# Casting loads in natural order, split first loads and a refitted schedule in a block-sparse attention kernel with a squared-ReLU MLP

## The chip, the cores and the metric

The kernel runs on one core of a Trainium2 chip. The metric is the device time of one launch in microseconds, lower is better; it is the median of three runs. The engines are TensorE (PE; its weight loads are listed as PEld), VectorE (DVE), ScalarE (ACT), GpSimd (POOL) and SyncE (SP), which here only issues DMAs. TensorE writes to PSUM, and DVE and ACT evacuate it from there.

## The reference

Two parts follow each other. The first is block-sparse attention over 4 batches x 8 heads, 768 tokens and head size 64; a query block of 32 tokens sees its neighbours, the first and the last block, three sampled blocks, and the first and last query block see everything. The second takes the 3072 x 512 result through two matrices with a squared ReLU between.

```python
scores = scale * np.matmul(q, k.transpose(0, 1, 3, 2))        # 4 x 8 x 768 x 768
...                                                            # mask from blocks of 32
scores = np.where(mask, scores, -1000000000.0)
attn = np.exp(scores - max)                                    # cut: the row maximum
attn = attn / (np.sum(attn, axis=-1, keepdims=True) + 1e-09)
x = np.matmul(attn, v)        # then heads side by side: 3072 x 512
...
h = x @ w_in                  # 3072 x 2048
r = np.maximum(h, 0.0)
out = (r * r) @ w_out         # 3072 x 512
```

## The kernel before

Heads are worked on in pairs: 16 pairs (u), four to a batch. A pair's q, k and v come as float32 of 384 KB each. For the first four pairs (batch 0) q and k are cast to bf16 by an engine (tile `qc`, with the two heads of a chunk of 128 tokens side by side), transposed on TensorE (tile `pt`) and evacuated to `QK`. For later pairs a DMA transposes them.

```python
    N_WARM = 12
    NRAW, NPB, QC_BUFS, XQ_BUFS = 4, 6, 5, 4
...
    sy.dma_start(out=sb_i, in_=sampled_blocks.bitcast(I32))
    load(0, (sy, sc_, sy))        # queues of q, k, v
    load(1, (sc_, sy, sc_))
    load(2, (sy, sc_, sy))
    load(3, (sc_, sy, sy))
...
    for _ in range(N_WARM):
        nc.tensor.matmul(junk, warm[:, 0:P], warm, start=True, stop=True)
...                               # POOL: iotas, one-hot rows oh, identity; DVE: mask bm
    def cast_qk(u, w, ns, e):
        c = work.tile([P, NCH, 2, D], BF, name="qc", tag="qc", bufs=QC_BUFS)[:, ns]
        copy(e, c, raw[u][w].rearrange("p t n d -> p n t d")[:, ns])

    def transp(u, w, ns, e):
        src = cast.pop((u, w, ns.start))
        pt = ps_h.tile([P, NCH, P], BF, name="pt", tag="h")
        for i, n in enumerate(range(ns.start, ns.stop)):
            nc.tensor.transpose(pt[:, n], src[:, i].rearrange("p t d -> p (t d)"), identb)

    def evac(u, w, ns, e):
        copy(e, QK[u % NPB][:, w]..., ttile.pop((u, w, ns.start))[:, ns])     # cut
```

A unit of attention is a slot: a pair, 256 queries and 256 keys. TensorE makes the scores (`ps`), two heads at once in two halves of the array's rows. ACT takes the exponential into `pT`. DVE multiplies by the 0/1 mask `MK`, and TensorE multiplies by v (`po`). The first twelve slots do without `MK`: TensorE adds mask rows (`R2`, evacuated from `pb`) to their scores. `MK` is made on TensorE (`pk`) in tiles of 512 and 256 columns.

```python
    def exps(a, e):
        A.activation(out=pT, in_=stile.pop(a), func=AF.Exp, scale=scale)
    def masks(a, e):
        V.tensor_tensor(out=pT, in0=pT, in1=m[:, None].broadcast_to([P, 2, 2, QW]), op=AOP.mult)
```

The result of a slot row is normalized on DVE (`rs`, `xq`), transposed to `xT`, and goes through the second part: `ph` (hidden), relu to `r` on DVE or ACT, square to `g` on GpSimd or ACT, `py` (output), copy to `ys`, store.

```python
    def hidden(T, f, half, e):                                   # ph: 4 matmuls of 256 or 384 columns
            nc.tensor.matmul(ph, w_in_sb[:, kc, f * P:(f + 1) * P], xT[b][:, kc, c0:c0 + w], ...)
    def output(T, ts, part, e):                                  # py: 16 matmuls of 512 columns
            nc.tensor.matmul(py, gtile[T, f][:, ts * P:(ts + 1) * P], w_out_sb[:, f, :], ...)
    def out_copy(T, ts, e):
        ys = work.tile([P, d_model], F32, name="ys", tag="ys", bufs=3)
        copy(e, ys, ytile.pop((T, ts)))
    def store(T, ts, e):
        sy.dma_start(out=ov[T[0], :, T[1] // P + ts, :], in_=ystile.pop((T, ts)))
```

No order of instructions is written by hand. While the program is built, `run_schedule` takes tasks with assumed durations, arrivals of loads and hand-over times, picks for each step the task that can start first, chooses its engine where more than one is allowed, and so fixes the order on every engine.

```python
    LAT = {"PE": 0.23, "DVE": 0.06, "ACT": 0.06, "POOL": 0.08, "SP": 2.0}
    SWITCH = 0.1
    AHEAD = {"PE": 0.05, "DVE": 0.2, "ACT": 0.25, "POOL": 0.0, "SP": 0.0}
    LEAD = 12.0
    PACE0, PACE, SINGLE, MASK_AT = 40.0, 1.6, 1, 12.0
...
    arrive = [(6.2, 6.2, 8.4), (8.4, 10.5, 10.5), (12.5, 12.5, 13.6), (13.6, 15.2, 16.3)]   # q, k, v of pairs 0 to 3
```

Of the kernel before, what the change touches and what calls it, by code (L numbers as in the profile page):

```python
# [19 lines left out]
P = 128  # L20
# [5 lines left out]
def kernel(  # L26
# [31 lines left out]
    N_WARM = 12  # L58
    NRAW, NPB, QC_BUFS, XQ_BUFS = 4, 6, 5, 4
# [19 lines left out]
    SWITCH = 0.1  # L79
    AHEAD = {"PE": 0.05, "DVE": 0.2, "ACT": 0.25, "POOL": 0.0, "SP": 0.0}  # L80
    LEAD = 12.0
    PACE0, PACE, SINGLE, MASK_AT = 40.0, 1.6, 1, 12.0
# [18 lines left out]
    def run_schedule(free, bufs, dma_free, mode=128):  # L101
        taken = {name: [] for name in bufs}
        port = {"DVE": (0.0, 0.0), "POOL": (0.0, 0.0)}
        waiting = list(tasks)
        ready = []

        def seen(d, eng):
            late = d.late if d.late is not None else (0.0 if d.eng == eng else LAT[d.eng])
            return d.end + late

        while waiting or ready:
# [6 lines left out]
            for t in ready:  # L118
# [15 lines left out]
                for e, us in t.engs.items():  # L134
                    r = max([r0, free[e]] + [seen(d, e) for d in t.deps])
                    sw = SWITCH if e == "PE" and t.mode and t.mode != mode else 0.0
                    if e == "POOL" or (e == "DVE" and t.port):
                        p0, p1 = port["DVE" if e == "POOL" else "POOL"]
                        us += 0.7 * max(0.0, min(r + us, p1) - max(r, p0))
# [12 lines left out]
            if e == "POOL" or (e == "DVE" and t.port):  # L152
                port[e] = (at, end)
            if e == "PE" and t.mode:
                mode = t.mode
# [34 lines left out]
    sy, sc_ = nc.sync, nc.scalar  # L190
    sb_i = consts.tile([nb, n_rand * 2], I32, name="sb_i")
    sy.dma_start(out=sb_i, in_=sampled_blocks.bitcast(I32))
    load(0, (sy, sc_, sy))
    load(1, (sc_, sy, sc_))
    load(2, (sy, sc_, sy))
    load(3, (sc_, sy, sy))
# [24 lines left out]
    G.iota(row, pattern=[[0, 1]], base=0, channel_multiplier=1, **small)  # L221
    o3 = oh.rearrange("a (n p) -> a n p", p=P)
# [12 lines left out]

    edge = consts.tile([nb, 2], F32, name="edge")
# [11 lines left out]
    A.copy(out=oh[D:P, :], in_=oh[0:D, :])  # L248
# [13 lines left out]
    def mask_rows(e):  # L262
        mtile["R"] = ps_s.tile([P, 1024], F32, name="pb", tag="ps")
        for c0 in (0, 512):
            w = min(512, S - c0)
            nc.tensor.matmul(mtile["R"][:, c0:c0 + w], bm, oh[0:nb, c0:c0 + w], start=True, stop=True)

    def mask_rows_evac(c0, c1, e):
        copy(e, R2[:, c0:c1], mtile["R"][:, c0:c1])
# [27 lines left out]
    def transp(u, w, ns, e):  # L297
        src = cast.pop((u, w, ns.start))
        pt = ps_h.tile([P, NCH, P], BF, name="pt", tag="h")
        for i, n in enumerate(range(ns.start, ns.stop)):  # L300
            nc.tensor.transpose(pt[:, n], src[:, i].rearrange("p t d -> p (t d)"), identb)  # L301
# [9 lines left out]
    held = consts.tile([1, 2], F32, name="held")  # L311
# [6 lines left out]
    def w_load(i, e):  # L318
        if i == 0:
            G.tensor_copy(out=held, in_=raw[2][1][0:1, 0, 0, 0:2])  # L320
# [127 lines left out]
    def y_pool(T, ts):  # L448
        return "h" if T == TILES[-1] and ts % 2 else "y"

    def output(T, ts, part, e):
        if part == 0:
            pool, tag = (ps_h, "h") if y_pool(T, ts) == "h" else (ps_y, "y")
            ytile[T, ts] = pool.tile([P, d_model], F32, name="py", tag=tag)
        py = ytile[T, ts]
        for f in range(part * NF // NY, (part + 1) * NF // NY):
            nc.tensor.matmul(py, gtile[T, f][:, ts * P:(ts + 1) * P], w_out_sb[:, f, :],  # L457
                             start=(f == 0), stop=(f == NF - 1))

    def out_copy(T, ts, e):  # L460
        ys = work.tile([P, d_model], F32, name="ys", tag="ys", bufs=3)
        copy(e, ys, ytile.pop((T, ts)))
        ystile[T, ts] = ys

    def store(T, ts, e):
        sy.dma_start(out=ov[T[0], :, T[1] // P + ts, :], in_=ystile.pop((T, ts)))
# [6 lines left out]
    arrive = [(6.2, 6.2, 8.4), (8.4, 10.5, 10.5), (12.5, 12.5, 13.6), (13.6, 15.2, 16.3)]  # L473
# [9 lines left out]
    def prepare(u):  # L483
# [5 lines left out]
        if u >= HP:  # L489
            g = gate[2] if u == HP else gate[5] if u == HP + 1 else gate[7]  # L490
            ld_t = T_(("SP", 1.3), s0 - 30, load, u, (sy, sy, sy),
                      deps=cv[u - NRAW] + tr[u - NRAW] + [g], dma=4.0)
# [7 lines left out]
        else:  # L500
            at = dict(after=arrive[u][2])
            for ns in (slice(0, 2), slice(2, NCH)) if u == 0 else (slice(0, NCH),):
                n = ns.stop - ns.start
                for w in (0, 1):
                    qc, hb = Buf("qc"), Buf("h")
                    opts = {"ACT": 0.23 + 0.1 * n} if u == 0 and w else {"DVE": 0.07 + 0.08 * n}
                    if u:
                        opts["POOL"] = 1.2
                    c = T_(opts, s0 - 6 + ns.start, cast_qk, u, w, ns, after=arrive[u][w], get=[qc], port=True)
                    tr[u].append(c)  # L510
                    t = T_(("PE", 0.06 * n), s0 - 5 + ns.start, transp, u, w, ns, deps=[c], get=[hb], put=[qc], mode=128)
                    opts = {"DVE": 0.14 + 0.07 * n}
                    if u == 0:
                        opts["ACT"] = 0.23 + 0.1 * n
                    x = T_(opts, s0 - 4 + ns.start, evac, u, w, ns, deps=[t], put=[hb])
                    for j in range(ns.start, ns.stop, 2):
                        ev[u][w, j] = x
            for w in (0, 1):
                ev[u].setdefault((w, 2), ev[u][w, 0])
        cv[u] = [T_({"POOL": 0.83, "DVE": 0.55}, s0 - 2 if u < HP else 101, cast_v, u, bias={"DVE": 0.6},  # L520
                    deps=at.get("deps", []) + old_v, after=at.get("after", 0.0), port=True)]
        if u == HP - 1:
            for i in range(2 * NWP):
                wl[i] = T_(("POOL", 0.85), -50 + i, w_load, i, after=12.6, late=2.2, dma=2.65)
# [3 lines left out]
    def attend(group, add):  # L528
# [4 lines left out]
                + (mr[:1 + (group[0][1] > 0)] if add else []) + sc_all[-1:], get=[bufs[a] for a in group], mode=64,  # L533
                after=PACE0 + PACE * (s - HP * NQ * CP) if s >= HP * NQ * CP else 0.0)
        sc_all.append(sc)
        for a in group:
# [9 lines left out]
            va = T_(("PE", 0.245), s + 2.2, values, a, deps=[ex] + cv[u] + va_all[-1:],  # L546
# [124 lines left out]
```

The softmax here doesn't subtract the row's maximum and nothing guards it: scores larger than these inputs give would overflow.

## Time and profile before

| | before |
|---|---|
| time, median of 3 | 281.56 us (281.35 to 282.2) |
| span of the profiled run | 279.6 us |
| exponential on ACT, 128x1024 | 144 x 1021 ns = 139.2 us busy |
| mask multiply on DVE, 128x1024 | 132 x 815 ns = 105.1 us busy |
| square on GpSimd | 107 x 889 ns = 94.5 us busy |
| first exponential starts | 8.92 us |
| first hidden matmul starts | 30.17 us |
| last matmul ends | 276.04 us |
| TensorE clock granted | full in every slice |

Matmuls are pipelined, so the busy time of TensorE counts overlapping work and a share of 96% doesn't mean that no time is lost; the distance between starts says more. The chain of waits follows the end of the program back from what released each step. An engine named in it is one that the next step had to wait for, or that had itself been busy until then. Idle time of an engine that nobody waits for costs nothing.

### The profile page before, as it was taken

Reading aid. Unit: us, or ns where it says so; the run is one execution under the profiler, and the core shown is the slowest. Engines: PE = TensorE matmul, PEld = TensorE weight load, DVE = VectorE, ACT = ScalarE, POOL = GpSimd, SP = SyncE. Lnnn points to the kernel's source line nnn. Section 1 sums busy time; section 2 is a strip of 40 time slices with the busy share of each in tenths; the row PEclk is TensorE's granted clock in tenths of the full one; section 3 lists DMA queues with packets and bytes.
Section 4 is the critical chain, followed back from the end, with each engine's and each line's share of the span. In section 5 each row is a group of like instructions: output and inputs, shape, how many; then the busy total and the mean of one; then the engine's idle time right before and its main releaser. Section 6 shows DMA issues by size and latency. Waiting matters only on the chain.

```text
span 279.6 us, 7039 instructions
## 1 busy us (share of the span) xinstructions
PE 267.9 (96%) x2834; PEld 155.6 (56%) x2834; DVE 200.4 (72%) x379; ACT 196.5 (70%) x281; POOL 122.1 (44%) x151
## 2 busy tenths in 40 slices
PE   7888899999999998999999999999999999999994
PEld 2565566566666554555555555555556555555541
DVE  6776889898988779986877888877868744344400
ACT  4689889899899799798988889889789501001011
POOL 4570358576434359752114443211120366666610
PEclk9999999999999999999999999999999999999999
DMA  7999997999933784794106314321011010111112
GB/s 249 378 228 207 269 277 239 195 285 258 357 65 83 237 193 120 213 191 106 56 12 115 81 45 111 70 59 49 19 51 56 12 47 38 40 39 38 40 74 76
DMA packets 50379, 36.89 MB, mean 132 GB/s; under 512 B 30891, under 2 KB 47275, under 8 KB 50347
## 3 DMA queue, kind: packets, MB, share of 16 engines
q1 hardware_dynamic: 44762, 30.29, 40.7%
q0 software_dynamic: 4224, 4.19, 9.0%
q10 hardware_dynamic: 1360, 1.97, 2.1%
q8 instruction: 22, 0.36, 0.6%
q14 instruction: 11, 0.08, 0.1%
HBM read 27.26 MB, written 6.29 MB: 120 GB/s over the span
## 4 chain that ended last, share of the span: by engine, by line
PE 78%; DVE 15%; ACT 4%; issue 2%; ACTq 0%; DVEq 0%
PE py L457 27%; PE ph L427 25%; PE po L382 12%; PE ps L349 11%; DVE pT L366 8%; DVE qc L172 3%; ACT pT L359 2%; DVE xq L391 2%; PE junk L213 2%; DVE rs L389 1%; DVE QK L172 1%; PE pt L301 1%; PE ps L353 0%; DVE r L436 0%; DVE xT L172 0%
## 5 line engine op out<-in xcount | busy, mean ns | idle before, releaser
L445 POOL TENSOR_TENSOR g<-r 128x384 bf16<-128x384 f32 (+1 forms) x107 | 94.5, 889 | 128.8 <-DVE r L436 93.0
L359 ACT ACTIVATE pT<-ps 128x1024 bf16<-128x1024 f32 x144 | 139.2, 1021 | 10.8 <-PE ps L349 7.6
L366 DVE TENSOR_TENSOR pT<-pT,MK 128x1024 bf16<-128x1024 bf16 x132 | 105.1, 815 | 9.0 <-ACT pT L359 8.7
L427 PE MATMUL ph<-xT,w_in_sb 128*128 128x384 bf16 (+1 forms) x576 | 107.8, 308 | 0.0
L457 PE MATMUL py<-w_out_sb,g 128*128 128x512 bf16 x384 | 103.5, 379 | 0.0
L427 PEld LDWEIGHTS <-w_in_sb 128*128 128x128 bf16 x576 | 51.1, 97 | 33.3 <-issue 3.4
L436 DVE TENSOR_SCALAR r<-ph 128x384 f32<-128x384 f32 (+1 forms) x80 | 41.9, 525 | 32.9 <-PE ph L427 22.2
L382 PEld LDWEIGHTS <-pT 128*128 128x128 bf16 x1152 | 45.8, 98 | 28.9 <-DVE pT L366 10.9
L382 PE MATMUL po<-VT,pT 128*128 128x65 bf16 x1152 | 56.5, 194 | 3.2 <-DVE pT L366 1.2
L457 PEld LDWEIGHTS <-g 128*128 128x128 bf16 x384 | 34.4, 98 | 25.7 <-issue 1.5
L170 ACT COPY ys<-py 128x512 f32<-128x512 f32 x21 | 12.3, 586 | 50.2 <-PE py L457 50.0
L349 PE MATMUL ps<-QK 64*128 64x256 bf16 x576 | 46.5, 272 | 1.0 <-ACT pT L359 0.8
L349 PEld LDWEIGHTS <-QK 64*128 64x128 bf16 x576 | 22.9, 94 | 21.2 <-issue 17.0
L434 ACT ACTIVATE r<-ph 128x384 f32<-128x384 f32 (+1 forms) x64 | 27.3, 451 | 6.7 <-PE ph L427 6.2
L443 ACT ACTIVATE g<-r 128x384 bf16<-128x384 f32 (+1 forms) x37 | 18.1, 489 | 6.4 <-DVE r L436 5.8
L391 DVE TENSOR_TENSOR xq<-po,rs 128x256 bf16<-128x256 f32 x48 | 20.4, 424 | 1.7
L172 POOL CAST VT<-vs 128x768 bf16<-128x768 f32 x15 | 14.8, 986 | 12.7 <-PE po L382 7.9
L389 DVE RECIPROCAL rs<-po 128x4 f32<-128x4 f32 x48 | 8.6, 179 | 14.9 <-PE po L382 14.7
L172 DVE CAST qc<-qs 128x768 bf16<-128x768 f32 (+2 forms) x15 | 10.2, 683 | 0.7 <-DMA qs<-in_q_dram 0.7
L172 DVE CAST qc<-ks 128x768 bf16<-128x768 f32 x14 | 10.5, 747 | 0.0
L353 PE MATMUL ps<-R,oh 64*128 64x256 bf16 x48 | 5.9, 269 | 0.0
L213 PE MATMUL junk<-warm 128*128 128x512 bf16 x12 | 4.4, 542 | 1.5 <-DVE warm L205 1.5
(52 smaller groups left out, 60.2 us busy)
## 6 DMA issues: line engine op xcount, KB each, us to landing
out_dram<-ys SPq DMA_DIRECT2D x24, 256.0 KB, 2.0
vs<-in_v_dram SPq DMA_DIRECT2D x15, 384.0 KB, 6.6
qs<-in_q_dram SPq DMA_DIRECT2D x14, 384.0 KB, 4.3
ks<-in_k_dram SPq DMA_DIRECT2D x14, 384.0 KB, 6.2
w_in_sb<-in_moe_w_in_dram POOLq DMA_DIRECT2D x4, 512.0 KB, 9.6
w_out_sb<-in_moe_w_out_dram POOLq DMA_DIRECT2D x4, 512.0 KB, 20.1
ks<-in_k_dram ACTq DMA_DIRECT2D x2, 384.0 KB, 6.2
qs<-in_q_dram ACTq DMA_DIRECT2D x2, 384.0 KB, 4.8
```

The source lines that it names most:

```text
L172: (V if e == "DVE" else G).tensor_copy(out=out, in_=in_)
L349: nc.tensor.matmul(ps[:, h, c, :], QK[i][hs, 1, ksl], QK[i][hs, 0, qsl], start=c == 0, stop=not add, skip_group_check=True)
L359: A.activation(out=pT, in_=stile.pop(a), func=AF.Exp, scale=scale)
L366: V.tensor_tensor(out=pT, in0=pT, in1=m[:, None].broadcast_to([P, 2, 2, QW]), op=AOP.mult)
L382: nc.tensor.matmul(po[:, qc, h, :], pT[:, h, c, qc * P:(qc + 1) * P], VT[i][:, h, n, 0:VW], start=(n == 0 and qc == 0 and h == 0), stop=n ...
L391: V.tensor_tensor(out=xq, in0=po[:, :, :, 0:D], in1=rs.broadcast_to([P, 2, 2, D]), op=AOP.mult)
L427: nc.tensor.matmul(ph, w_in_sb[:, kc, f * P:(f + 1) * P], xT[b][:, kc, c0:c0 + w], start=(kc == 0), stop=(kc == KM - 1))
L434: A.activation(out=r, in_=src, func=AF.Relu)
L436: V.tensor_scalar(out=r, in0=src, scalar1=0.0, scalar2=None, op0=AOP.max)
L443: A.activation(out=g, in_=r, func=AF.Square)
L445: (G if e == "POOL" else V).tensor_mul(out=g, in0=r, in1=r)
L457: nc.tensor.matmul(py, gtile[T, f][:, ts * P:(ts + 1) * P], w_out_sb[:, f, :], start=(f == 0), stop=(f == NF - 1))
```

## The change

- Pairs 1 to 3: q and k are no longer cast by engines. DMAs issued by GpSimd cast while they load, into six tiles `nat` that keep the order of memory (head, chunk, 64 values). So the two heads of a chunk don't lie side by side, and TensorE transposes each head's 64 columns by itself, into the upper or lower half of `pt`: twice as many transposes, half as wide. Their v follows on the SP queue, each after a tiny DMA that waits until the pair's q has landed. `qs`, `ks` and `vs` need one buffer less.
- First pair: q and k are loaded in two parts, the first two chunks and then the other four, so that the first scores need a third of the bytes.
- The weights' first load no longer waits for a load of pair 2.
- Last tokens: the output of the last 128 tokens is made in two halves of 256 columns, so that the first half is copied and stored while the second is made.
- Scheduler: nine warm-up matmuls instead of twelve; new arrivals, hand-over times and pace; contention of DVE and GpSimd now lengthens the earlier task too; a slack of 0.1 us where TensorE waits for another engine; squares are kept off ACT more strongly; the evacuation of the later mask rows and the mask tiles of 256 columns move later.

```diff
-    N_WARM = 12
-    NRAW, NPB, QC_BUFS, XQ_BUFS = 4, 6, 5, 4
+    N_WARM = 9
+    NRAW, NPB, QC_BUFS, XQ_BUFS, YS_BUFS = 3, 6, 5, 4, 3
@@ scheduler
-    SWITCH = 0.1
-    AHEAD = {"PE": 0.05, "DVE": 0.2, "ACT": 0.25, "POOL": 0.0, "SP": 0.0}
-    LEAD = 12.0
-    PACE0, PACE, SINGLE, MASK_AT = 40.0, 1.6, 1, 12.0
+    SWITCH, SHARE, SLACK = 0.096, 0.6, 0.1
+    AHEAD = {"PE": 0.03, "DVE": 0, "ACT": 0.1, "POOL": 0.0, "SP": 0.0}
+    LEAD = 8
+    PACE0, PACE, SINGLE, MASK_AT, ADDED = 36, 1.589, 1, 15.0, 0
...
-            return d.end + late
+            return d.end + late + (SLACK if eng == "PE" and d.eng != "PE" else 0.0)
@@ loads
+    def load_first():
...
+        for ns in SPLIT:                  # chunks 0 to 1, then 2 to 5
+            cs = slice(ns.start * D, ns.stop * D)
+            for eng, t, view in ((sy, qs, qv), (sc_, ks, kv)):
+                eng.dma_start(out=t[:, :, ns].rearrange("p t n d -> p t (n d)"), in_=view[0, 0][:, :, cs])
+        sy.dma_start(out=vs.rearrange("p t n d -> p t (n d)"), in_=vv[0, 0])
+
+    def load_cast(u, w):
+        t = consts.tile([P, 2, NCH, D], BF, name=f"nat{u}{w}")
+        G.dma_start(out=t.rearrange("p t n d -> p t (n d)"), in_=(qv, kv)[w][0, u])
+
+    def load_v(u, e):
+        sy.dma_start(out=scratch[0:1, u:u + 1], in_=nat[u, 0][0:1, 0, 0, 0:1])
+        t = ld.tile([P, 2, NCH, D], F32, name="vs", tag="vs")
+        sy.dma_start(out=t.rearrange("p t n d -> p t (n d)"), in_=vv[0, u])
...
-    load(0, (sy, sc_, sy))
-    load(1, (sc_, sy, sc_))
-    load(2, (sy, sc_, sy))
-    load(3, (sc_, sy, sy))
+    load_first()
...                                        # POOL: after the iotas
+    load_cast(1, 0)
+    load_cast(1, 1)
...                                        # POOL: after one-hot rows, identity, ones of VT
+    for u in range(2, HP):
+        for w in range(2):
+            load_cast(u, w)
@@ transposes
-            nc.tensor.transpose(pt[:, n], src[:, i].rearrange("p t d -> p (t d)"), identb)
+            if u == 0:
+                nc.tensor.transpose(pt[:, n], src[:, i].rearrange("p t d -> p (t d)"), identb)
+            for t in range(2) if u else ():
+                nc.tensor.transpose(pt[t * D:(t + 1) * D, n], src[:, t, n], identb)
@@ weights
-        if i == 0:
-            G.tensor_copy(out=held, in_=raw[2][1][0:1, 0, 0, 0:2])
@@ last tokens
+    HALVES = ((0, d_model // 2), (d_model // 2, d_model))
...
+        return ys[:-1] + [(n - 1, cs) for cs in HALVES] if T == TILES[-1] else ys
@@ tasks
-    arrive = [(6.2, 6.2, 8.4), (8.4, 10.5, 10.5), (12.5, 12.5, 13.6), (13.6, 15.2, 16.3)]
+    arrive = [(4.6, 4.6, 8.2), (7.6, 9.1, 12.3), (10.4, 12.1, 15.0), (13.5, 14.8, 17.0)]
...
-                wl[i] = T_(("POOL", 0.85), -50 + i, w_load, i, after=12.6, late=2.2, dma=2.65)
+                wl[i] = T_(("POOL", 0.85), -50 + i, w_load, i, after=9.5 + 1.5 * i, late=2.2, dma=2.65)
...
-            va = T_(("PE", 0.245), s + 2.2, values, a, deps=[ex] + cv[u] + va_all[-1:],
+            va = T_(("PE", 0.245), s + 3.2, values, a, deps=[ex] + cv[u] + va_all[-1:],
...
-            for c0, c1, at in ((QW, S, MASK_AT), (0, QW, 26.0)):
+            for c0, c1, at in ((QW, S, MASK_AT), (0, QW, 38.0)):
...
-                rr = T_(RELU[w], 200, relu, t, f, deps=[h1], get=[rb], put=[hb], bias={"ACT": 0.4})
-                sq_of[x] = T_(SQ[w], n_key, square, t, f, deps=[rr], get=[gb], put=[rb], bias={"ACT": 0.5})
+                rr = T_(RELU[w], 200, relu, t, f, deps=[h1], get=[rb], put=[hb], bias={"ACT": 0.3})
+                sq_of[x] = T_(SQ[w], n_key, square, t, f, deps=[rr], get=[gb], put=[rb], bias={"ACT": 0.9})
```

## The prediction

> **What bounds the kernel now.** I read the share of busy time first, then busy time in stretches, then the chain of waits for the first 31 us, then the order of time around the start and the end. The page's first part and the stretches:
>
> ```profile
> PE 267.9 (96%) x2834; PEld 155.6 (56%) x2834; DVE 200.4 (72%) x379; ACT 196.5 (70%) x281; POOL 122.1 (44%) x151
> ```
>
> ```profile
> 20.00:25.00 5.00, 4.60 (x75) 2.78 (x74) 2.88 (x6) 4.87 (x7) 0.00 (x0) 1.00 1.25 209
> 25.00:30.00 5.00, 3.71 (x65) 2.26 (x61) 4.24 (x10) 3.92 (x7) 0.00 (x0) 1.00 1.20 229
> ...
> 80.00:100.00 20.00, 20.00 (x250) 12.76 (x250) 15.82 (x34) 17.30 (x23) 7.17 (x9) 1.00 0.50 134
> ...
> 200.00:250.00 50.00, 50.00 (x405) 27.67 (x404) 29.52 (x56) 21.41 (x31) 22.27 (x26) 1.00 0.13 41
> ```
>
> The columns of a stretch are its length, then PE, PE weight load, DVE, ACT and GpSimd with their counts, the clock, the DMA share and GB/s. From about 80 us on TensorE is full. What the kernel can gain without removing matmuls lies in the first 30 us, in some holes between 30 and 125 us, and after the last matmul. Two chains of waits and one piece of the timeline show the sizes (start, length, what):
>
> ```profile
> 1.53 4.39 PE junk L213 x12
> 5.92 0.44 PE pb L266 x2
> 6.38 0.38 ACT R L170
> 6.79 0.69 DVE R L172
> 7.48 0.21 DVE QK L172
> ...
> 24.65 0.85 PE po L382 x24
> 29.69 0.54 PE ps L349 x8
> 30.23 0.56 PE ph L427 x4
> ...
> 110.01 1.17 DVE qc L172
> ...
> 264.58 0.65 PE ph L427 x4
> 265.24 10.80 PE py L457 x50
> 276.11 0.58 ACT ys L170
> ```
>
> ```profile
> 8.92 2.85 ACT L359 ACTIVATE pT<-ps 128x1024 bf16<-128x1024 f32 x3 [1.65 <-PE ps L353]
> ```
>
> The reader sees four things. Three instructions on ACT and DVE (the mask rows R, then the first evacuation into QK) stand between the warm-up and the first scores. ACT's first exponential starts at 8.92. The first hidden matmul (ph), the work with which TensorE fills every later hole, starts only at 30.2. And the last matmul ends at 276.04, so 279.6 - 276.04 = 3.56 us are copy and store.
>
> How much of the first 30 us is idle on TensorE is worked out from the pace of matmuls in these rows: po 0.85/24 = 0.035 us, ps 0.54 for a group of eight with its change of tiling, ph of 384 columns 0.65/4 = 0.162, py 10.80/50 = 0.216. Before 30.17 us the program holds 12 single score groups with mask rows (four pairs at 0.11 plus a change, 0.54 each: 6.5), 3 double groups (1.6), 120 po (4.2), 48 transposes at about 0.06 (0.35 for six in the chain: 2.9), 8 transposes of xq (0.5), mask tiles (6 x 0.216 + 6 x 0.108 = 1.9) and pb (0.4): 18.0 us. From 5.85 to 30.17 are 24.3 us. So 6.3 us are lost there.
>
> [...] the DMA share is 1.05 to 1.25 in every stretch from 5 to 30 us, whichever queue fed it. [...] the weights already are, at 0.87 us of GpSimd each (the row of w_in_sb, 869 ns in the mean). [...] The new transposes, two of 64 columns to one chunk, are of that shape; the trace of before has none, and shows only the row case (score pairs 0.11 us apart with 0.27 us each). [...] The warm-up's weight loads, 0.43 us apart until 4.9 us and closer after it, agree, so nine instead of twelve still cover it. [...] The mask multiply takes 0.68 us where GpSimd is idle (26.09 us) and 815 ns in the mean.
>
> **The change part by part.**
>
> First pair. The first loads shrink from 384 KB each for q, k and v to 128 KB of q and of k. In before, q landed at 5.8 us. With a third of the bytes I take about 4.5, so the loads no longer decide. Now DVE's mask arithmetic does (bm is ready at 5.14) and GpSimd's identity, which moves behind two cast-load issues: 4.74 + 2 x 0.87 less the 1.1 us that GpSimd idled, about 5.4. Then, in the new order: transpose of k 5.4, cast of q 5.14 to 5.43, QK of k about 6.0, R 256 (0.37) and R 512 (0.69) to 7.1, QK of q (0.28) to 7.4, scores, first exponential about 8.0. That is 0.9 earlier than 8.92.
>
> Pairs 1 to 3. Six casts leave the compute engines (in before 0.55 to 0.84 us each on DVE between 8.8 and 15.8 us: about 3.8 us), and one v cast goes to GpSimd. Their chain is now landing, transpose, evacuation. Evacuations stay: 3.2 us for six, now split into nine (0.28 + 0.42 for 0.55, three times: +0.5). GpSimd issues six loads (6 x 0.87 = 5.2 us) before its first v cast, which so ends near 10 us instead of 8.9; the first values follow the third score group, at about 10, as before. On TensorE, 36 transposes of 128x128 (2.2 us) become 72 of 64x128: 2.2 us if the two halves overlap as the score pairs do, 4.3 if not.
>
> First hidden matmul. ACT runs 7 exponentials, a mask tile, 2, a mask tile, 3: 12 x 0.97 (7.78/8 in before) + 2 x 0.60 from 8.0 gives 20.8 us for the last single. In the new order, two masked slots precede ph: a mask tile and two more exponentials to 23.4, mask multiply 0.68, values 0.4: 24.6. TensorE's own work before it (18.0 less one double group and the six small mask tiles, with the new transposes) is 16.8 to 18.9 us, from 5.3 to 22.1 to 24.2, so it doesn't bind by itself. With 0.6 us for stalls ph starts at 25.3, not 30.2. What was put off, one double group 0.54 and six mask tiles of 256 columns 0.65, has to be done later: 1.2. Net gain 4.9 - 1.2 = 3.7 us.
>
> Refit of the scheduler. The counts by engine are the same but for 22 squares which go from ACT to GpSimd (6 of 256 columns, 16 of 384: ACT -6 x 0.417 - 16 x 0.523 = -10.9 us; GpSimd +6 x 0.81 + 16 x 0.93 = +19.7 us), three more relus of 384 columns on ACT instead of DVE, and fewer copies on ACT. TensorE's work is the same, so only holes can change. In 40 to 60 us TensorE is 18.98 of 20 busy, in 100 to 150 it is 48.46 of 50: 2.6 us, in both cases with DVE on the chain (the cast at 110.01 above, 1.17 us). I give the refit 1.0 of these, and 1.5 either way.
>
> Last tokens. 32 matmuls of 256 columns for 16 of 512: no change. The last copy is of 128x256: about 0.40 (the relu of that shape takes 0.399 on ACT) for 0.58; the store is half as large, its landing of 2.0 us mostly fixed: 0.1. Gain 0.3.
>
> Sum: 281.56 - 3.7 - 1.0 - 0.3 = 276.56, taken as 276.5.
>
> **The rivals.**
>
> The cast loads are late. [...] the new order of TensorE puts a transpose of pair 1's q before the second score group, in program order. If it lands at 10 instead of 8 to 9 us, TensorE, and behind it ACT, stand still, and the same can happen at pairs 2 and 3. For it: the DMA share is already over 1, and a weight piece took 9.6 us to land. Against: up to pair 1 only about 1.97 MB are asked for (four parts of pair 0, its v, and q and k of pair 1), and 370 GB/s, as between 5 and 8 us, moves that in 5.3 us from about 2.7. If true, 2 to 3 us of the 3.7 go: about 279.
>
> DVE and ACT take over. In 40 to 60 us DVE is 18.50 and ACT 18.29 of 20 busy, and 30 to 70 us of the chain run over DVE's mask multiply. An earlier start only helps if that stage also starts earlier, and 19.7 us more of GpSimd beside DVE lengthen the multiply. If half of the squares met a multiply and each cost it 0.15 us, DVE gains 1.6 us of work in stages with little room: about 278.
>
> The whole gain is kept and the holes close. If ph starts at 24.6 and the refit closes 2.5 us: 281.56 - 4.4 - 2.5 - 0.3 = 274.4.
>
> New stalls from a fit that misses the chip: the order of every engine is fixed by a model, and a wrong arrival stops TensorE in order. 280 to 283.
>
> **Range and chances.** 2% is 275.93, 0.6 us below my figure, so the first two chances are close. The uncertain terms are the start (+-1.5), the refit (+-1.5) and the transposes (up to 2.1, off the path if ACT leads). Together about 2.4 us of spread: 273.6 to 280.2 holds eight in ten. Faster by over 2%: 0.42. Within: 0.54. Slower: 0.04.
>
> **What would show it.** Right: first exponential near 8.0, first ph near 25, no DVE cast before 30 us, TensorE without holes over 1 us from 25 on, 3.2 to 3.3 us after the last matmul. Wrong: transposes of nat waiting for a DMA, 64-column transposes 0.06 us apart, a mask multiply mean well over 815 ns, DVE-ended waits of TensorE around 100 to 125 us as large as before, or ph near 25 and yet an end near 280, which would mean that DVE or ACT sets the pace between.

## The result and the profile after

| | before | after |
|---|---|---|
| time, median (lowest to highest) | 281.88 us (281.35 to 282.37, 4 runs) | 277.36 us (276.71 to 278.55, 4 runs) |
| span of the profiled run | 279.6 us | 275.4 us |
| first exponential starts | 8.92 us | 8.62 us |
| 12th exponential starts | 23.2 us | 22.8 us |
| first hidden matmul (ph) starts | 30.17 us | 27.93 us |
| 1st, 48th, 64th, 144th relu | 30.8, 93.1, 124.8, 265.3 us | 28.6, 90.3, 119.9, 261.6 us |
| last copy to the end of the span | 3.5 us | 3.0 us |

The ratio is 0.9845, 95% interval 0.9804 to 0.9885: faster, by less than 2%.

The first part of the page after shows what moved between engines. GpSimd gained the squares (and issues more DMAs), ACT lost them, and DVE is where it was:

```profile
PE 264.2 (96%) x2845; PEld 157.1 (57%) x2883; DVE 199.5 (72%) x375; ACT 187.4 (68%) x261; POOL 152.1 (55%) x178
```

Busy time in stretches of the kernel after (columns as in the prediction; the third number from the end is the granted clock of TensorE):

```profile
5.00:8.00 3.00, 1.37 (x13) 0.72 (x13) 2.69 (x8) 1.38 (x2) 2.93 (x12) 0.97 1.18 254
8.00:11.00 3.00, 2.91 (x28) 1.66 (x26) 1.15 (x4) 1.02 (x1) 2.75 (x4) 0.50 1.18 160
11.00:14.00 3.00, 3.00 (x58) 2.10 (x56) 0.85 (x2) 2.74 (x3) 0.00 (x0) 0.96 1.13 233
...
40.00:60.00 20.00, 19.07 (x256) 12.70 (x258) 19.04 (x35) 18.94 (x34) 13.00 (x15) 1.00 1.04 280
100.00:125.00 25.00, 24.52 (x278) 13.92 (x279) 21.68 (x36) 24.02 (x37) 15.46 (x16) 1.00 0.79 199
```

In the second line TensorE is "busy" for 2.91 of 3 us and issues 28 matmuls, where the kernel before issued 47 in the same three microseconds: its granted clock (its share of full speed) is 0.50. Before had 1.00 there. The last line is the gain further on: before had 23.46 of 25 us busy in that stretch.

The chain of waits of the kernel after, from DVE's mask arithmetic to the first hidden product (start, length, what):

```profile
4.05 0.93 DVE al L284
...
5.86 0.51 PE pb L303 x2
6.39 1.02 DVE R L182 x2
7.41 0.21 DVE QK L182
7.66 0.29 PE ps L387 x2
7.95 0.21 PE ps L391 x2
8.16 0.21 PE ps L387 x2
...
11.81 0.11 PE ps L391 x2
11.92 0.11 PE ps L387 x2
...
14.16 0.46 PE pt L342 x12
...
22.61 0.13 PE ps L391 x2
22.82 1.02 ACT pT L397
...
24.30 1.03 ACT pT L397
25.35 0.69 DVE pT L404
...
28.09 0.87 PE ph L465 x8
```

Three things are read from it. Between 8.59 and 22.61 nearly every piece is TensorE's own (ps, pt, po, pk; the one exception is a copy into QK at 9.16): ACT isn't on the chain there, and its own waits in that stretch end with ps. Pairs of score matmuls that follow one another are 0.21 us apart until 11.0 and 0.11 after it, the halved clock in another view (the first pair behind other work takes 0.21 at full clock too, as at 12.72). At 0.11 us apart each pair is listed with 0.27 us, so they overlap. And twelve transposes of 64 columns take 0.46 us, 0.038 each, nearer to the 0.03 that the prediction gave for overlapping halves than to 0.06.

### The profile page after: what moved, and what is told of

It is laid out like the page before. It is cut to its first block, busy times and chain, and to the rows that moved or that the text cites. A ratio compares the mean times of both kernels' runs of the same rounds, so it can differ in the third digit from the quotient of the medians.

```text
span 275.4 us, 7159 instructions
## 1 busy us (share of the span) xinstructions
PE 264.2 (96%) x2845; PEld 157.1 (57%) x2883; DVE 199.5 (72%) x375; ACT 187.4 (68%) x261; POOL 152.1 (55%) x178
## 4 chain that ended last, share of the span: by engine, by line
PE 82%; DVE 10%; DMA 2%; issue 2%; POOL 2%; ACT 1%; ACTq 0%; DVEq 0%; POOLq 0%
PE py L505 27%; PE ph L465 26%; PE po L420 12%; PE ps L387 12%; DVE pT L404 4%; DMA xT<-xq 2%; POOL g L483 2%; PE pt L342 1%; PE ps L391 1%; DVE xq L429 1%; DVE qc L182 1%; DVE r L474 1%; ACT pT L397 1%; PE pk L313 1%; PE po L436 1%
## 5 line engine op out<-in xcount | busy, mean ns | idle before, releaser
L483 POOL TENSOR_TENSOR g<-r 128x384 bf16<-128x384 f32 (+1 forms) x129 | 121.7, 949 | 92.0 <-DVE r L474 58.1
L404 DVE TENSOR_TENSOR pT<-pT,MK 128x1024 bf16<-128x1024 bf16 x132 | 107.2, 834 | 7.5 <-ACT pT L397 7.2
L465 PE MATMUL ph<-xT,w_in_sb 128*128 128x384 bf16 (+1 forms) x576 | 109.8, 308 | 0.3
L505 PE MATMUL py<-w_out_sb,g 128*128 128x512 bf16 (+1 forms) x362 | 96.6, 370 | 2.0 <-issue 0.5
L420 PEld LDWEIGHTS <-pT 128*128 128x128 bf16 x1152 | 47.6, 98 | 25.4 <-issue 7.4
L180 ACT COPY ys<-py 128x512 f32<-128x512 f32 (+1 forms) x23 | 13.1, 568 | 49.2 <-PE py L505 49.1
L387 PEld LDWEIGHTS <-QK 64*128 64x128 bf16 x576 | 22.9, 94 | 25.6 <-issue 22.8
L472 ACT ACTIVATE r<-ph 128x384 f32<-128x384 f32 (+1 forms) x67 | 29.1, 451 | 11.0 <-PE ph L465 10.9
L182 DVE COPY QK<-pt 128x256 bf16<-128x256 bf16 (+2 forms) x13 | 5.1, 399 | 5.2 <-PE pt L342 3.8
L182 DVE CAST qc<-ks 128x768 bf16<-128x768 f32 x11 | 8.7, 795 | 0.0
L481 ACT ACTIVATE g<-r 128x384 bf16<-128x384 f32 (+1 forms) x15 | 7.2, 482 | 0.5
```

Source lines behind the costliest of these rows:

```text
L180: A.copy(out=out, in_=in_)
L182: (V if e == "DVE" else G).tensor_copy(out=out, in_=in_)
L387: nc.tensor.matmul(ps[:, h, c, :], QK[i][hs, 1, ksl], QK[i][hs, 0, qsl], start=c == 0, stop=not add, skip_group_check=True)
L420: nc.tensor.matmul(po[:, qc, h, :], pT[:, h, c, qc * P:(qc + 1) * P], VT[i][:, h, n, 0:VW], start=(n == 0 and qc == 0 and h == 0), stop=n ...
L472: A.activation(out=r, in_=src, func=AF.Relu)
L483: (G if e == "POOL" else V).tensor_mul(out=g, in0=r, in1=r)
```

## The experiments

A time is given as a median over its runs. The kernel before ran beside each of them and had 281.7 to 282.0; the ratio is to it, with its 95% interval.

### The clock: e1, e10, e11

Theory: TensorE's clock falls between 8 and 11 us because of the idle time just ahead, and the slow matmuls cost a microsecond of the start. Rival: nine warm-up matmuls are too few, wherever they stand.

**e1**, twelve warm-up matmuls in the changed kernel:

```diff
-    N_WARM = 9
+    N_WARM = 12
```

> The changed kernel with twelve warm-up matmuls instead of nine, all else and every other order the same. In the changed kernel the granted clock is 0.97 from 5 to 8 us and 0.50 from 8 to 11 us, and score pairs there lie 0.21 us apart instead of 0.11. Theory A (the missing three warm-up matmuls let the clock drop): clock 1.00 from 8 to 11, second exponential at about 9.7 instead of 11.1, twelfth at about 21.5 instead of 22.8, and 0.8 to 1.5 us less in all, 276.2 against 277.4. Theory B (the clock drops because TensorE waits from 6.4 to 7.7 us for the mask rows, whatever came before): still 0.50 there, time unchanged or 0.4 us longer because the warm-up ends at 5.9 and holds the first transposes.

Measured: 275.86 us, ratio 0.9792 (0.9763 to 0.9822). The clock was 1.00 from 5 to 14 us in its profile. The mean clock was 1.00 in five of six runs, which took 275.4 to 276.2 us; the sixth had 0.994 and took 277.67. The claim of the prediction that nine "still cover it", so that TensorE is at full clock behind them, is refuted. The wait ahead of the first scores is as long as in the changed kernel, 1.09 us (6.98 to 8.07), so it doesn't halve the clock by itself. But twelve end later, and the first queries' transposes follow them directly, where the changed kernel has another 0.42 us of idle time. So this run alone doesn't tell theory and rival apart.

**e10**, nine warm-up matmuls as in the changed kernel, and four more where TensorE stood idle:

```diff
+        if (u, w, ns.start) == (0, 0, 0):      # behind the first queries' transposes
+            more = ps_y.tile([P, d_model], F32, name="py", tag="y")
+            for _ in range(N_FILL):                # 4
+                nc.tensor.matmul(more, warm[:, 0:P], warm, start=True, stop=True)
```

> The changed kernel with its nine warm-up matmuls, and four more 128x512 matmuls of the same kind behind the transposes of the first queries, where TensorE stood idle from 6.4 to 7.7 us; their result isn't used. If the granted clock fell to 0.50 between 8 and 11 us because of that idle stretch and not because of the number of warm-up matmuls ahead of it, the clock stays at 1.00 there, the score pairs come 0.11 us apart again, and the time is near the twelve-matmul version's (275.9). If the missing three warm-up matmuls count by themselves, the clock falls as before and the time stays at 276.9 to 277.4, or above it should the four matmuls delay the first scores.

Measured: 275.61 us (275.07 to 276.66), ratio 0.9781 (0.9758 to 0.9804). The timeline of TensorE in e10 (start, length, what) has the four at 6.41, and the scores start where they started in the changed kernel (7.66), but 0.11 us apart:

```profile
6.41 1.03 PE L348 MATMUL py<-warm 128*128 128x512 bf16 x4
7.67 0.28 PE L392 MATMUL ps<-QK 64*128 64x256 bf16 x2 [0.23 <-DVE QK L183]
7.77 0.29 PE L396 MATMUL ps<-R,oh 64*128 64x256 bf16 x2
```

And the stretches of e10, to be laid beside those of the kernel after:

```profile
5.00:8.00 3.00, 2.75 (x19) 1.11 (x18) 2.72 (x8) 1.39 (x2) 2.93 (x12) 1.00 1.23 254
8.00:11.00 3.00, 2.81 (x49) 1.68 (x44) 2.22 (x5) 2.01 (x2) 2.88 (x4) 1.00 1.18 232
```

49 matmuls instead of 28 between 8 and 11 us. The twelfth exponential starts at 21.64 instead of 22.82, the first ph at 26.76 instead of 27.93. Nothing else was changed, and nothing that is computed depends on the four.

**e11**, the kernel before with nine warm-up matmuls:

```diff
-    N_WARM = 12
+    N_WARM = 9
```

> The kernel before with nine warm-up matmuls instead of twelve. If nine are too few only in the new order, in which TensorE waits 1.1 us for the first queries, the clock stays at 1.00 and the time within 0.2 us of 281.8. If nine are too few in any order, the clock falls below 1.00 between 8 and 14 us, the first hidden product comes 0.5 to 1 us later and the time goes to about 282.5.

Measured: 281.60 us, ratio 0.9992 (0.9976 to 1.0008). Its stretch from 8 to 11 us, and TensorE's timeline there:

```profile
8.00:11.00 3.00, 3.00 (x29) 1.94 (x26) 1.32 (x3) 1.30 (x2) 1.74 (x2) 1.00 1.06 374
```

```profile
8.62 0.39 PE L349 MATMUL ps<-QK 64*128 64x256 bf16 x2
8.81 0.42 PE L353 MATMUL ps<-R,oh 64*128 64x256 bf16 x2
9.03 0.42 PE L349 MATMUL ps<-QK 64*128 64x256 bf16 x2
...
11.04 0.28 PE L349 MATMUL ps<-QK 64*128 64x256 bf16 x2
11.16 0.27 PE L353 MATMUL ps<-R,oh 64*128 64x256 bf16 x2
11.27 0.27 PE L349 MATMUL ps<-QK 64*128 64x256 bf16 x2
```

The column says a clock of 1.00, the pace says half of it: the score pairs are 0.21 us apart from 8.62 to 10.09, and 0.11 from 11.04 on. The clock record of this trace begins only at 10.81 us (in before at 4.86), and the stretches count time without a record as 1.00. The warm-up agrees with the pace: its last matmuls start 0.43 us apart, up to 4.91, where those of before are 0.22 us apart from 4.89 on. So in this execution nine were too few in the old order as well. The first ph came at 31.29, 1.1 us later than in before, and this run took 282.21 us, 0.7 more than before's profiled run. The rival doesn't fall. The median of twelve runs shows no loss, so what nine cost in the old order stays open.

Nor are twelve always enough. e6, further down, has twelve, and its clock is 0.50 from 9.79 to 13.20 us. The 3.41 us ahead of that (6.38 to 9.79) have 1.96 us of work on TensorE and no gap over 0.73.

So what is shown is this: in the new order, more matmuls ahead of the first scores keep the pace, behind the warm-up (e1) or in the wait (e10). Neither the number of warm-up matmuls nor the longest gap tells by itself whether the clock halves. Nor does the same kernel do it at a fixed time: the stretch at 0.50 begins at 7.82 us in after and at 9.26 in e5, the same kernel again. Seven traces have a fall on record, and in the 3.41 us ahead of it (as long as the stretch at 0.50 in after, 7.82 to 11.23) TensorE is busy for 1.2 to 2.1 us (1.78 in after). In e1, from 5.49 to 8.90, it is busy for 2.32 us, and in e10, from 5.82 to 9.23, for 2.97; no fall follows. But none follows in e3 either, after a stretch with 1.62 (19.25 to 22.66), so no rule in terms of busy time is shown.

The gain in time is near what the profiles say, 1.2 us at the first ph and about 1.5 us in the medians. It isn't seen in every single run: of eight runs of the changed kernel, seven had a mean clock of 0.992 to 0.994 and 276.2 to 277.6 us, and one had 1.00 and 278.55. A mean of 1.00 can be a gap in the record, as e11 shows; whether it is one here stays open.

### Loads and order: e2, e3, e6, e7

Theory: the casting loads take work from DVE, the refit closes the holes behind, and the two add. Rival: neither is worth anything without the other, since the order on each engine was fitted to the arrivals.

**e2**, the changed kernel with q and k of pairs 1 to 3 loaded as float32 and cast by engines, as before (the weights' first load waits for pair 2 again); first loads in parts, halves and scheduler stay:

```diff
-    load_cast(1, 0)                       # and the five others
+    load(1, (sc_, sy, sc_))               # and pairs 2 and 3, behind load_first()
-            for t in range(2) if u else ():
-                nc.tensor.transpose(pt[t * D:(t + 1) * D, n], src[:, t, n], identb)
+            nc.tensor.transpose(pt[:, n], src[:, i].rearrange("p t d -> p (t d)"), identb)
```

> The changed kernel with pairs 1 to 3 loaded and cast as before the change (float32 loads on SP and ACT, casts by DVE or GpSimd, 36 wide transposes); the split first load, the halves and the refit stay. Theory A (the casting loads make the earlier start of the second part): first hidden matmul back at about 30, last relu 2 us later than in the changed kernel, 279.3 us. Theory B (the refit makes most of it): first hidden matmul within 1 us of 28.1 and the time within 0.7 us of 277.4.

Measured: 282.74 us, ratio 1.0027 (1.0009 to 1.0045). This is more than either expectation gave. First exponential 9.2, fourth 15.8 (13.3 in the changed kernel), twelfth 25.2. TensorE's timeline in e2 names DVE's cast and the evacuation behind it:

```profile
14.04 0.51 PE L338 MATMUL pt<-identb,qc 128*128 128x128 bf16 x6 [0.50 <-DVE qc L182]
...
15.20 0.28 PE L389 MATMUL ps<-QK 64*128 64x256 bf16 x2 [0.33 <-DVE QK L182]
```

**e6**, all the loads as before, twelve warm-up matmuls, with the new scheduler and the halves:

```diff
-    load_first()                          # and the six load_cast
+    load(0, (sy, sc_, sy))                # and pairs 1 to 3; arrivals, casts and transposes as before
-    N_WARM = 9
+    N_WARM = 12
```

> All loads, casts and transposes as before the change, twelve warm-up matmuls, arrivals as before, but the new scheduler (constants, slack, longer earlier task, later mask tiles, biases) and the halves. Theory A (the refit is a gain by itself): 279.5 us or less. Theory B (the refit is only worth something with the new loads): 281 us or more, with the 64th relu at 124 us or later.

Measured: 281.12 us, ratio 0.9976 (0.9961 to 0.9991). Refit and halves without the new loads are worth 0.7 us of the 4.5. Part of what is missing may be the clock, at 0.50 from 9.79 to 13.20 us in this trace: the four of its sixteen runs with a mean clock of 0.999 or 1.00 took 279.8 to 280.8 us, the others 280.7 to 282.7. The traces of e2 and e3 have such a fall too.

**e3**, the new loads with the old scheduler constants, and **e7**, the same with twelve warm-up matmuls:

```diff
-    SWITCH, SHARE, SLACK = 0.096, 0.6, 0.1
-    AHEAD = {"PE": 0.03, "DVE": 0, "ACT": 0.1, "POOL": 0.0, "SP": 0.0}
-    LEAD = 8
-    PACE0, PACE, SINGLE, MASK_AT, ADDED = 36, 1.589, 1, 15.0, 0
+    SWITCH, SHARE, SLACK = 0.1, 0.7, 0.0
+    AHEAD = {"PE": 0.05, "DVE": 0.2, "ACT": 0.25, "POOL": 0.0, "SP": 0.0}
+    LEAD = 12.0
+    PACE0, PACE, SINGLE, MASK_AT, ADDED = 40.0, 1.6, 1, 12.0, 0
...                               # also s + 2.2, 26.0, the two bias values, and no lengthening
...                               # of the earlier task, as before;
...                               # e7 besides: N_WARM = 12 for 9
```

> The changed kernel with the constants of the scheduler as before the change (pace, hand-over, slack, biases of relu and square, times of the mask tiles, no lengthening of the earlier task); loads, halves and nine warm-up matmuls stay. Theory A (the start makes the gain): 278.0 us or less. Theory B (the refit makes at least half of the 4.5 us): 279.5 us or more, with the 64th relu at about 124 instead of 119.9 and the first at about 28.6.

> The changed kernel with the old constants of the scheduler as in the earlier run, now with twelve warm-up matmuls so that the clock isn't in play. With nine it took 285.3 us, and its first relu came at 35.3 us. If the late first relu is the doing of the order (a v cast on DVE that waits for the v of pair 3 until 22.1 us, then mask tiles and mask multiplies in front of the normalization): again 284 us or more, first relu at 34 to 35 us. If it was the clock: 282 us or less.

Measured: e3 285.25 us, ratio 1.0111 (1.0080 to 1.0143); e7 286.46 us, ratio 1.0150 (1.0122 to 1.0178). Both are slower than the kernel before. DVE's timeline in e7 shows one wait that does much of it (in brackets the idle time ahead and what ended it):

```profile
17.86 0.42 DVE L182 COPY QK<-pt 128x512 bf16<-128x512 bf16 x1 [0.24 <-PE pt L342]
22.51 0.84 DVE L182 CAST VT<-vs 128x768 bf16<-128x768 f32 x1 [4.23 <-DMA vs<-in_v_dram]
23.27 0.16 DVE L427 RECIPROCAL rs<-po 128x4 f32<-128x4 f32 x1
23.47 0.42 DVE L429 TENSOR_TENSOR xq<-po,rs 128x256 bf16<-128x256 f32 x1
```

and the chain of waits of e3 leads back through the same instruction to GpSimd's issues:

```profile
7.04 7.59 DMA nat<-in_q_dram
14.65 0.24 SPq L219
...
15.00 7.14 DMA vs<-in_v_dram
...
22.16 0.56 DVE VT L182
```

In the order that the old constants give, the v cast of pair 3 stands on DVE ahead of the normalization (rs, xq). So in e7 DVE does nothing for 4.23 us, and TensorE waits 3.80 us for xq (2.46 in e3). During this wait e7's clock falls, and it is at 0.50 from 22.4 to 29.2 us, in spite of the twelve warm-up matmuls. The first relu comes at 35.3 (e3) and 38.1 us (e7), 6.7 and 9.5 later than in the changed kernel; for e3 28.6 had been expected even if the refit made half of the gain. What else adds to the delay wasn't followed up. So the rival holds, and more strongly than stated: in the four corners, old loads and old order have 281.8, old loads and new order 281.1, new loads and old order 285.3 to 286.5, both new 276.9 to 277.4.

### Who waits for v: e8

**e8**, twelve warm-up matmuls, and the v casts of pairs 1 to 3 allowed on DVE alone:

```diff
-        cv[u] = [T_({"POOL": 0.83, "DVE": 0.55}, ...
+        cv[u] = [T_({"DVE": 0.55} if 0 < u < HP else {"POOL": 0.83, "DVE": 0.55}, ...
```

> Twelve warm-up matmuls, and the v casts of pairs 1 to 3 only on DVE, so that GpSimd issues all eight weight loads one after the other from about 9.3 us instead of stopping at three v casts that wait for their loads until 14.7, 19.3 and 21.7 us. If the late weights hold TensorE (in the run with twelve it waited for w_out from 39.5 to 40.15 us): all issued by 16 us, last w_out gate at 41 to 42 us instead of 43.8, and 0.5 to 1 us less than with twelve, 275.0. If the DMA engines are the limit and only the order among loads changes: gates within 0.7 us of before, v of pairs 1 to 3 land 2 to 4 us later, DVE waits for them, and the time is the same or up to 3 us more.

Measured: 279.77 us, ratio 0.9930 (0.9908 to 0.9952), 3.9 us more than with the casts on GpSimd (e1). The waits on DVE in e8:

```profile
14.80 0.56 DVE L182 CAST VT<-vs 128x768 bf16<-128x768 f32 x1 [2.29 <-DMA vs<-in_v_dram]
...
18.65 0.56 DVE L182 CAST VT<-vs 128x768 bf16<-128x768 f32 x1 [1.75 <-DMA vs<-in_v_dram]
...
21.89 0.56 DVE L182 CAST VT<-vs 128x768 bf16<-128x768 f32 x1 [0.84 <-DMA vs<-in_v_dram]
```

and the same casts on GpSimd in e1, which differs by this edit alone:

```profile
14.72 0.82 POOL L182 CAST VT<-vs 128x768 bf16<-128x768 f32 x1 [3.95 <-DMA vs<-in_v_dram]
...
19.34 0.82 POOL L182 CAST VT<-vs 128x768 bf16<-128x768 f32 x1 [2.38 <-DMA vs<-in_v_dram]
...
21.73 0.82 POOL L182 CAST VT<-vs 128x768 bf16<-128x768 f32 x1
```

The casts start within 0.7 us of the same times, whoever waits; v landed no later, where 2 to 4 us had been expected. Behind them on GpSimd stand only weight loads; on DVE the waits hold up the rest, and the time is 3.9 us longer. In e8 the weight loads were issued from 9.9 to 15.8 us, in e1 from 9.3 to 23.2, and yet the gates for the weights passed at 25.5, 36.8 and 42.9 us, where e1 has 26.5, 37.2 and 43.8. A lead of up to 7.4 us in issuing became 0.4 to 1.0 us in landing, so GpSimd's queue was hardly what held the weights. What did hold them wasn't shown; the DMA share was 1.13 to 1.20 from 5 to 14 us in e1, and 1.13 to 1.24 from 5 to 30 us in after.

### The first scores, and the best version: e9, e12

DVE copies the later mask rows (R, 128x512, 0.64 us) ahead of the first queries, for which TensorE waits. **e9** has twelve warm-up matmuls and the two copies exchanged:

```diff
+        if c0 and not q_ready:            # later mask rows: kept back
+            held.append((c0, c1, e)); return
         copy(e, R2[:, c0:c1], mtile["R"][:, d0:d0 + c1 - c0])
...
+        if (u, w, ns.start) == (0, 0, 0): # first queries are in QK: now
+            for a in held: mask_rows_evac(*a)
```

> Twelve warm-up matmuls as in the version at 275.86, and on VectorE the copy of the two later query chunks' mask rows (R, 128x512, 0.64 us) stands behind the copy of the first queries (QK, 128x256) instead of ahead of it; nothing else moves. If the time is set by when the hidden products start (profiled time minus the first relu has been 248.0 to 249.5 in every version with the new loads), the first scores begin about 0.6 us earlier (first exponential 8.1), the first relu comes at about 27.2, and the time is 275.2. Rival: the start is caught up by later waits (for w_out's gate near 40 us, for VectorE between 40 and 60 us), and it stays at 275.9.

Measured: 275.65 us, ratio 0.9782 (0.9762 to 0.9802). The first scores began 0.35 us earlier than in e1 (7.72 for 8.07), but the first relu stayed at 27.8. **e12** joins it to e10, with two filling matmuls and nine warm-up matmuls:

```diff
+            for _ in range(N_FILL):            # 2, behind the first queries' transposes
+                nc.tensor.matmul(more, warm[:, 0:P], warm, start=True, stop=True)
...                                            # and the exchange of e9
```

> Nine warm-up matmuls, two filling 128x512 matmuls (0.43 us) behind the transposes of the first queries, and the copy of the later mask rows (R, 128x512) behind that of the first queries. Both gains are small by themselves (275.61 with four filling matmuls, 275.65 with the copy moved). If they add, the first scores begin at about 7.0 us, the first exponential at 7.7, the first relu at about 27.0, and the time is 275.2. Rival: what the first exponential gains is lost before the twelfth (TensorE's own work and the loads of pairs 1 to 3 are the limit from 9 us on), the first relu stays at 27.4 and the time at 275.6.

Measured: 275.50 us (274.76 to 277.14), ratio 0.9777 (0.9750 to 0.9805). The first exponential starts at 7.7 as expected, the fourth at 12.3, later than e10's 12.1, and the first relu comes at 27.5 (e10: 27.4). Where the 0.6 us went that its first exponential is ahead of e10's, TensorE's timeline says:

```profile
11.38 0.30 PE L347 MATMUL pt<-identb,nat 128*64 128x128 bf16 x4 [0.66 <-DMA nat<-in_q_dram]
```

It is the wait of the prediction's first rival, for a casting load. The changed kernel, which comes to that transpose at 12.49, doesn't have it, nor has e10 at 11.25; e9 has 0.24 us of it. The expected rival is right: from 9 us on the loads and TensorE's own work set the pace. e12, e10 and e9 aren't told apart by their intervals; any of them is 6.3 to 6.5 us faster than the kernel before, and around the 2% mark.

### Halves, and the changed kernel again: e4, e5

**e4** makes the last tokens' output in one piece:

```diff
-        return ys[:-1] + [(n - 1, cs) for cs in HALVES] if T == TILES[-1] else ys
+        return ys
```

> The changed kernel with the last 128 tokens in one piece of 512 columns. The tail after the last matmul was 3.56 us before and 3.1 us in the changed kernel. If the halves make that difference: last matmul to end of span 3.5 us, and 0.4 to 0.5 us more in all, 277.8 us. If not: within 0.2 us of 277.4.

Measured: 277.59 us, ratio 0.9855 (0.9830 to 0.9880). In the profiles the last copy's start to the end of the span is 3.6 us without halves (copy 0.58, 256 KB) and 3.0 with them (copy 0.37, 128 KB; the last stores of 256 KB take 2.0 us to land in before, those of 128 KB 1.7 in after), so the halves are worth some 0.5 us there; in the times the difference is 0.2 us and inside the intervals.

**e5** is the changed kernel again, without an edit:

> The changed kernel once more, unchanged, beside the next three. In the first four runs the twelve warm-up matmuls came to 275.9 us and the changed kernel had been 277.4 us, but their profiles are alike at the 48th exponential (74.2 and 74.1 us) and the 64th relu (119.9 and 119.8), and part only where one DMA transpose of xq took 6.48 us to land in the changed kernel's profile. Theory A (the clock drop costs the time): 277.0 us or more again, ratio to before 0.983 to 0.987. Theory B (the difference was in DMA landing times and the drop is absorbed by 48 us): 276.0 to 276.8 us, within 0.7 us of the run with twelve.

Measured: 276.90 us (276.24 to 277.08), ratio 0.9818 (0.9797 to 0.9839), beside the first 277.36. This lies between the two expectations and decides for neither; e10 does.

### One rule over all runs

The profiled time less the start of the first relu is nearly a constant for each way of loading:

| new loads | e1 | e3 | e4 | e5 | e7 | e8 | e9 | e10 | e12 | after |
|---|---|---|---|---|---|---|---|---|---|---|
| first relu, us | 27.8 | 35.3 | 28.6 | 28.8 | 38.1 | 30.9 | 27.8 | 27.4 | 27.5 | 28.6 |
| time less that, us | 248.4 | 249.5 | 248.9 | 248.1 | 249.0 | 248.4 | 248.4 | 248.2 | 248.3 | 248.5 |

With the old loads it is 250.3 to 251.5 (before, e2, e6, e11). The first relu varies by 10.7 us and the rest by 1.4, so what delays that point is paid nearly in full. A reason that fits: from the first hidden products on TensorE has work for the holes and little idle time (in e10 it is 20.00 of 20 us busy from 80 to 100).

The rest also shows where the two parts add and where they don't. The versions differ in how much of TensorE's work ahead of the first ph they have moved behind it: against before, after moved 8 score matmuls, 8 value matmuls and 6 mask tiles, e6 moved 8, 16 and 6, e3 and e7 none. At the paces of the prediction (0.54 us for a group of eight score matmuls, 0.035 for a value matmul, 0.108 for a mask tile) that is 1.5 us in after and 1.75 in e6. An estimate of the rest without this work is 250.7 us in before, about 249 with the new order alone (e6), 249.0 to 249.5 with the new loads alone (e7, e3), and 247.0 with both; all but before have the halves, some 0.5 us. So behind the start each part gains something by itself, as far as single profiles show. It is at the start that they don't add: there the new loads in the old order lose 4.5 to 7.3 us.

## The prediction, step by step

The time, 276.5 predicted and 277.36 measured, came out of errors of opposite sign; that it lies so near is luck. In the terms of its sum, with the spans of the two profiles (279.6 and 275.4, a gain of 4.2):

| term | predicted | measured |
|---|---|---|
| start: first ph earlier, less work put off | 4.9 - 1.2 = 3.7 | 2.2 - 1.5 = 0.7 |
| refit, between the first ph and the last copy | 1.0 | 4.2 - 0.7 - 0.5 = 3.0 |
| last tokens | 0.3 | 0.5 |
| sum | 5.0 | 4.2 |

The work put off is 1.5 and not 1.2, since the prediction left out the eight value matmuls (8 x 0.035 = 0.28). The refit is what is left over.

**First exponential**: predicted 8.0, measured 8.62. Two sub-steps failed. The mask bm was taken over from the trace of before at 5.14; it came at 5.80. DVE's comparison at 4.05 ran beside a GpSimd select that the two issues ahead of it had moved there. Both engines' timelines after (start, length):

```profile
4.05 0.92 DVE L284 TENSOR_TENSOR al<-col,sb_i 24x72 f32<-24x72 f32 x1
```

```profile
4.04 0.86 POOL L257 TENSOR_SCALAR_AFFINE_SELECT oh<-oh 128x768 bf16<-128x768 bf16 x1
```

In before the select had ended at about 4.1, and the comparison took 0.21 us beside a smaller one, of 128x128. Some 0.4 us of the delay lie there; the rest is bm's own instruction, 0.45 us for 0.18, and no run shows why. That the select lengthened the comparison, 0.92 for 0.21 us, is read from these two traces alone; no experiment moved the select away. The other 0.3 us are the clock: with e10's filling the first exponential is at 8.31.

**Nine warm-up matmuls "still cover it"**: wrong, as e1 and e10 show, and in e11's trace they don't cover it in the old order either. It was an estimate from the pace of before's warm-up (weight loads 0.43 us apart until 4.9 us) and didn't ask what TensorE does in the microseconds after them.

**Twelfth exponential and first ph**: this is the largest error. The prediction paced ACT back to back, which puts the twelfth start at 8.0 + 11 x 0.97 + 2 x 0.60 = 19.9. It was at 22.8, 2.9 later: 1.2 are the clock (e10: 21.64), 0.3 the remaining delay of the first exponential, and the 1.4 that are left are put down to TensorE's own work. "So it doesn't bind by itself" failed because the sum of TensorE's work up to ph was compared with the end of the stretch and not with each point in it: in e10, at full clock, TensorE works from 7.67 to 21.6 with 0.2 us idle before the twelfth scores are made, and ACT needs 11.9 of these 13.9 us. From there to ph, 5.1 us in after against 5.4 predicted, the step holds.

**Transposes of 64 columns**: 0.038 us each, inside the given bounds (0.03 to 0.06), and near the overlapped end of it.

**Refit**: right in kind and too small. The wait for DVE's cast near 110 us is gone as a hole; TensorE's idle time from 40 to 60 and 100 to 125 us together was 2.6 us and is 1.4 in after (1.0 in e10). The other 1.8 of the 3.0 isn't pinned to a hole and stays open. And the term doesn't exist alone: e6 shows 0.7 us for order and halves without the loads. That the two parts depend on each other at the start is the thing the sum was blind to.

**Rivals.** Late casting loads: landing took 5.9 (q) and 6.7 us (k) in the median, and TensorE didn't wait for them in after, only in e7, e9 and e12 (0.26, 0.24 and 0.66 us), which get there earlier. DVE and ACT as the bound: between 40 and 60 us DVE is busy for 19.04 of 20 us and the mask multiply rose from 815 to 834 ns in the mean (0.68 to 0.69 us in both traces where the timelines show no GpSimd instruction beside it), 132 x 0.019 = 2.5 us of DVE's time against the 1.6 supposed. So this rival was right about DVE, but wrong that the start would then be lost: the rest stays within 1.4 us for first relus from 27.4 to 38.1 us. A misfit of the order: not in the change, but it is what e3 and e7 are, at 285.3 and 286.5, beyond even the 283 given for it.

## What to carry to other kernels

Find the point from which the bounding engine has filling work for every hole, and count what delays that point: here nearly every microsecond ahead of it was paid in full. In a program whose order is fixed in advance, a new way of loading and the order fitted to it are one change; put a cast that waits for a DMA on an engine that has nothing urgent behind it. After moving instructions, look again at the granted clock in the first stretches and check it against the distance between like matmuls, since the record of the clock can have gaps (in e11 it begins at 10.81 us). And compare each engine's work with the pace of the others at every point and not only as a total.

## What the runs showed of the hardware

- TensorE's clock halved (0.50 from 7.82 to 11.23 us in after) behind 3.41 us in which it was busy for 1.78, the longest gap being 1.09 us. Four filling matmuls of 128x512 in that gap kept it at 1.00. In e6 it halved behind 3.41 us with 1.96 busy and no gap over 0.73. In e7 it halved from 22.4 to 29.2 us, behind 3.41 us with 1.18 busy.
- The clock column can be 1.00 where nothing was recorded: in e11 the score pairs from 8.62 to 10.09 us are 0.21 us apart, twice the usual 0.11, at a column of 1.00.
- A DVE comparison of 24x72 elements took 0.92 us beside a GpSimd select of 128x768, and 0.21 beside one of 128x128.
- Issuing the last of the weight loads 7.4 us earlier (e8 against e1) let the last gate pass 0.9 us earlier. The DMA share was 1.13 to 1.20 from 5 to 14 us in e1.
- In the chain of waits of the kernel after, the piece of one DMA transpose of xq is 6.48 us long, where the median from issue to landing is 2.4. The four ph matmuls behind it take 1.07 us, for 0.81 in e5, so TensorE lost about 0.26 us. The chains of e1 and e5 don't pass through it, and what lengthened it wasn't tried.

```profile
114.73 6.48 DMA xT<-xq
...
121.25 0.34 PE ph L465
```
